# Eight state products of a chunk, written to four groups of PSUM partitions, and four copies that bring them to the next chunk

## The chip, the cores and the metric

The kernel runs on one core of a Trainium2 chip. The metric is the device time of one execution in microseconds, as the median of several runs. Each run starts from inputs in device memory and ends when the output is there.

## The reference

Two stages follow one another. The first is a state-space scan over 4 batches, 8 heads and 768 positions, with head width D = 32 and state width N = 16. Within a chunk, with `cum` the running sum of log a:

```python
L = np.exp(cum[:, :, :, None] - cum[:, :, None, :]) * causal
M = np.einsum('bhin,bhjn->bhij', Cc, Bc) * L
y = np.einsum('bhij,bhjd->bhid', M, xc) + y_inter(state)
state = decay_full * state + sum_j(Bc[j] x xc[j] * decay_from_j)
```

The second takes the scan's result as 3072 tokens of 256 values through a feed-forward layer with 2048 hidden units: `h = x @ w_in`, `g = h - tanh(h)`, `out = g @ w_out`. Everything is float32.

## The kernel before, in words

**Chunks of the scan.** The kernel cuts the 768 positions of a batch into seven chunks, six of Q = 112 positions and a last one of 96, which makes 28 chunks in all. A chunk's x tile has 128 rows (partitions): rows 0 to 15 hold the state that the chunk before left, and rows 16 to 127 its own positions. So the state enters a chunk as sixteen more rows of x, and one product over 128 rows gives both the part from the chunk and the part from the state. For each chunk:

- `chunk_a` (in the first token tile, `first_tile`) has PE compute the decay sums and the products C·B into the PSUM tile `att` (L405, L411; L346 and L357 in the first tile), ACT take the exponential into `lt` (L415, L364), DVE multiply the two (L419, L369) and GpSimd set what is not causal to zero (L422, L374).
- `chunk_y` has PE multiply `lt` and x into the PSUM tile `y` (L446): eight products, one for each head. Head h of each group of four goes to partitions 32h to 32h + 31, so that the four lie in four groups of partitions. If the chunk isn't the last of its batch, eight more products of b and x follow (L451), one for each head, 128 rows, 16 output partitions and 32 columns: the state that the next chunk needs. All eight go to partitions 0 to 15, side by side in columns 256 to 511 of `y`. 24 of the 28 chunks have them.
- Three instructions read `y`: ACT copies the state, 16 partitions and 256 columns, to rows 0 to 15 of the next chunk's x (`fn_c`, L455); ACT rounds y to float32r as `xh` (`fn_h`, L461); DVE takes the rest y - xh as `xl` (`fn_l`, L466). `y` has one buffer, so the next chunk's products wait until these are done.

**The feed-forward layer.** It works on twelve tiles of 256 tokens and eight slices of 256 hidden units (`mm1`, `act`, `mm2`). Each product is split into a high and a low part: `mm1` (L491) does xh·wh, xh·wl and xl·wh into `ph`; ACT takes the Tanh (L505), DVE subtracts (L509), ACT rounds g to gh (L513), DVE takes the rest gl (L520), and `mm2` (L541) sums three products into `o`. The weights are brought into their high and low parts by `conv` (L261 to L285) on ACT and DVE, slice by slice, beside the work on the first four token tiles. `mm2` runs two steps behind `mm1`.

**The order.** Nothing is issued as it is written down. Each piece of work is an entry `op(engine, cost, fn, r, w)` in a list, with the names that it reads and writes. `Order.schedule` then simulates the engines with the costs given and `Order.issue` does so in 16 rounds with priorities that a seeded random generator shifts by a little, one draw per entry, and issues all entries in the order of the shortest simulated span. Each engine works through its own queue in that order.

Of the kernel before, what the change touches and what calls it, by code (L numbers as in the profile page):

```python
# [21 lines left out]
NB, H, S, D, N = 4, 8, 768, 32, 16  # L22
# [10 lines left out]
CPG = 2  # L33
# [14 lines left out]
class Order:  # L48
# [12 lines left out]
    def slot(self, tag, bufs):  # L61
        k = self.count[tag] = self.count.get(tag, -1) + 1
        self.fresh[f"{tag}#{k}"] = tag, f"{tag}#{k - bufs}"
        return f"{tag}#{k}"
# [107 lines left out]
def tile_ssm_moe(ctx: ExitStack, tc: tile.TileContext, a, x, bn, bc, wts, out):  # L172
    nc = tc.nc
# [10 lines left out]
    op = Order()  # L184
    slot = op.slot
    grp = {g: {} for g in range(NG)}
# [4 lines left out]
    for t in range(NT):  # L191
        b, j = divmod(t, S // TT)
# [129 lines left out]
    def qlen(ck):  # L322
        return QL if ck % CPB == CPB - 1 else Q
# [13 lines left out]
    def first_tile():  # L337
# [39 lines left out]
        for ck in range(len(chunks[0])):  # L377
            k = chs[ck]
            k["n_l"] = op.pieces(slot("lt", NL), 2)
            if ck % CPG == 0:  # L380
                prep(ck // CPG)
            for i in range(2):
                n_f = slot("ph", NPH)
                op("PE", 0.9, lambda ck=ck, i=i: fn_f(ck, i), r=["la", "upto"], w=[n_f])
                op("ACT", 1.0, lambda ck=ck, i=i: fn_x(ck, i), r=[n_f, "ncum", "tab"], w=[k["n_l"][i]])
                if i == 0:
                    op("PE", 0.55, lambda ck=ck: fn_p(ck), r=[grp[ck // CPG]["n_bc"]], w=[n_a[ck % 2]])
                op("DVE", 0.6, lambda ck=ck, i=i: fn_m(ck, i), r=[n_a[ck % 2]], w=[k["n_l"][i]])
                op("POOL", 0.6, lambda ck=ck, i=i: fn_s(ck, i), w=[k["n_l"][i]])
            chunk_y(ck)  # L390
# [39 lines left out]
    def chunk_y(ck):  # L430

        d, k, q = grp[ck // CPG], chs[ck], qlen(ck)
        b, c = divmod(ck, CPB)
        cg = ck % CPG
        n_y = slot("y", 1)
        last = c == CPB - 1
        if c == 0:
            seq[b]["n_xh"] = op.pieces(slot("xh", 2), CPB)
            seq[b]["n_xl"] = op.pieces(slot("xl", 2), CPB)
        n_xh, n_xl = seq[b]["n_xh"][c], seq[b]["n_xl"][c]  # L440

        def fn():
            y = k["y"] = ps_y.tile([P, 2 * H * D], F32, tag="y", name=f"y{ck}")
            for hg in range(2):
                for h in range(4):
                    nc.tensor.matmul(out=y[D * h : D * h + D, hg * Q : hg * Q + q],  # L446
                                     lhsT=d["x"][:, cg, P * hg + D * h : P * hg + D * h + D],
                                     rhs=k["l"][:, 4 * hg + h, 0:q], start=True, stop=True)
            if not last:
                for h in range(H):  # L450
                    nc.tensor.matmul(out=y[0:N, H * D + D * h : H * D + D * h + D], lhsT=d["b"][:, cg, N * h : N * h + N],  # L451
                                     rhs=d["x"][:, cg, D * h : D * h + D], start=True, stop=True)

        def fn_c():
            nc.scalar.copy(grp[(ck + 1) // CPG]["x"][0:N, (ck + 1) % CPG], k["y"][0:N, H * D : 2 * H * D])  # L455

        def fn_h():
            if c == 0:
                seq[b]["xh"] = p3.tile([P, 2, S], F32R, tag="xh", name=f"xh{b}", bufs=2)
            k["yv"] = k["y"][:, 0 : 2 * Q].rearrange("p (g q) -> p g q", g=2)[:, :, 0:q]  # L460
            nc.scalar.copy(seq[b]["xh"][:, :, c * Q : c * Q + q], k["yv"])  # L461

        def fn_l():
            if c == 0:
                seq[b]["xl"] = p3.tile([P, 2, S], F32R, tag="xl", name=f"xl{b}", bufs=2)
            nc.vector.tensor_tensor(out=seq[b]["xl"][:, :, c * Q : c * Q + q], in0=k["yv"],  # L466
                                    in1=seq[b]["xh"][:, :, c * Q : c * Q + q].bitcast(F32), op=ALU.subtract)

        op("PE", 0.5 if last else 1.0, fn, r=[*k["n_l"], d["p_x"][cg], d["n_b"]], w=[n_y])
        if not last:  # L470
            op("ACT", 0.35, fn_c, r=[n_y], w=[grp[(ck + 1) // CPG]["p_x"][(ck + 1) % CPG]])
        op("ACT", 0.36, fn_h, r=[n_y], w=[n_xh])
        op("DVE", 0.4, fn_l, r=[n_y, n_xh], w=[n_xl])

# [244 lines left out]
    for i in range(4):  # L719
# [5 lines left out]
       r=[n_pq2], w=["wdec"])  # L725
# [31 lines left out]
    for ck in at_:  # L757
        plan(at_[ck][0], chunk_a, ck)
        plan(at_[ck][1], chunk_y, ck)
        if (ck + 1) % CPG == 0 and ck // CPG + NGB < NG:  # L760
            plan(at_[ck][1], group, ck // CPG + NGB)
# [58 lines left out]
```

## Time and profile before

| | us |
|---|---|
| median of 3 runs | 357.83 (356.96 to 358.04) |
| profiled execution, its own time | 358.88 |
| its span, first to last instruction | 356.9 |
| PE busy | 344.9 (97%) |
| DVE busy | 230.7 (65%) |
| ACT busy | 181.9 (51%) |
| POOL busy | 58.0 (16%) |

A page of the profile and the views of its trace all show one execution. Engines are PE (matrix products; PEld is the loading of their weights), DVE, ACT, POOL (GpSimd) and SP, which issues most DMAs. A float32 product shows as two MATMUL records and two weight loads, so that the eight state products of a chunk are 16 records. Records of PE overlap, since a product starts while the one before still runs out; busy time is the union. L451 is line 451 of the kernel.

### The profile page before, as it was taken

Reading aid. Unit: us, or ns where it says so; the run is one execution under the profiler, and the core shown is the slowest. Engines: PE = TensorE matmul, PEld = TensorE weight load, DVE = VectorE, ACT = ScalarE, POOL = GpSimd, SP = SyncE. Lnnn points to the kernel's source line nnn. Section 1 sums busy time; section 2 is a strip of 40 time slices with the busy share of each in tenths; the row PEclk is TensorE's granted clock in tenths of the full one; section 3 lists DMA queues with packets and bytes.
Section 4 is the critical chain, followed back from the end, with each engine's and each line's share of the span. In section 5 each row is a group of like instructions: output and inputs, shape, how many; then the busy total and the mean of one; then the engine's idle time right before and its main releaser. Section 6 shows DMA issues by size and latency. Waiting matters only on the chain.

```text
span 356.9 us, 8786 instructions
## 1 busy us (share of the span) xinstructions
PE 344.9 (97%) x3756; PEld 331.7 (93%) x3756; DVE 230.7 (65%) x335; ACT 181.9 (51%) x343; POOL 58.0 (16%) x69
## 2 busy tenths in 40 slices
PE   7795999999999999999999999999999999999995
PEld 6695889999999999999999999999999999999995
DVE  4879899999889665645655554644645554644552
ACT  4555687875545344355454544544544444544441
POOL 2063545401100000120211210210121110110000
PEclk9998799999999999999999999999999999999999
DMA  8877483540100001011110300300300000000000
GB/s 229 202 177 192 138 264 101 172 137 0 44 3 0 2 31 60 31 42 32 57 44 12 91 3 0 90 13 2 99 4 1 31 3 2 31 0 2 29 2 29
DMA packets 12438, 21.42 MB, mean 60 GB/s; under 512 B 2876, under 2 KB 7628, under 8 KB 12388
## 3 DMA queue, kind: packets, MB, share of 16 engines
q1 hardware_dynamic: 11824, 18.78, 18.7%
q10 hardware_dynamic: 576, 2.10, 2.0%
q8 instruction: 29, 0.48, 0.6%
q14 instruction: 9, 0.07, 0.1%
HBM read 17.55 MB, written 3.32 MB: 58 GB/s over the span
## 4 chain that ended last, share of the span: by engine, by line
PE 91%; DMA 3%; DVE 3%; ACT 1%; issue 1%; SPq 0%; ACTq 0%
PE o L541 40%; PE ph L491 38%; PE y L446 4%; DMA bc<-bc_d 3%; PE att L411 3%; PE y L451 3%; PE cp L346 2%; PE att L405 1%; DVE lt L419 1%; DVE wm L274 0%; DVE wv L278 0%; DVE lt L369 0%; PE att L357 0%; ACT wv L261 0%; DVE xl L466 0%
## 5 line engine op out<-in xcount | busy, mean ns | idle before, releaser
L509 DVE TENSOR_TENSOR g<-ph,g 128x512 f32<-128x512 f32 x96 | 66.0, 689 | 68.2 <-ACT g L505 68.1
L505 ACT ACTIVATE g<-ph 128x512 f32<-128x512 f32 x96 | 57.4, 598 | 103.4 <-PE ph L491 97.5
L491 PE MATMUL ph<-xh,wh 128*128 128x256 f32 x384 | 100.6, 284 | 0.0
L491 PE MATMUL ph<-xh,wl 128*128 128x256 f32 x384 | 99.5, 281 | 0.0
L520 DVE TENSOR_TENSOR gl<-g,gh 128x512 fp32r<-128x512 f32 x96 | 66.6, 696 | 23.8 <-ACT gh L513 21.3
L491 PE MATMUL ph<-xl,wh 128*128 128x256 f32 x384 | 76.6, 280 | 0.0
L491 PEld LDWEIGHTS ph<-xh,wh 128*128 128x128 f32 x384 | 72.6, 189 | 1.0 <-issue 0.2
L513 ACT CAST gh<-g 128x512 fp32r<-128x512 f32 x96 | 59.2, 617 | 27.5 <-DVE g L509 26.3
L491 PEld LDWEIGHTS ph<-xh,wl 128*128 128x128 f32 x384 | 72.6, 189 | 0.0
L422 POOL TENSOR_SCALAR_AFFINE_SELECT lt<-lt 128x896 f32<-128x896 f32 (+1 forms) x25 | 31.5, 1260 | 218.5 <-DVE lt L419 218.5
L541 PE MATMUL o<-gh,wh 128*128 128x256 f32 x384 | 64.0, 288 | 0.0
L541 PE MATMUL o<-gl,wh 128*128 128x256 f32 x384 | 60.7, 279 | 0.0
L541 PE MATMUL o<-gh,wl 128*128 128x256 f32 x384 | 60.6, 279 | 0.0
L491 PEld LDWEIGHTS ph<-xl,wh 128*128 128x128 f32 x384 | 59.1, 189 | 0.0
L541 PEld LDWEIGHTS o<-gh,wh 128*128 128x128 f32 x384 | 51.6, 188 | 2.7
L541 PEld LDWEIGHTS o<-gl,wh 128*128 128x128 f32 x384 | 51.9, 188 | 0.0
L541 PEld LDWEIGHTS o<-gh,wl 128*128 128x128 f32 x384 | 51.9, 187 | 0.0
L419 DVE TENSOR_TENSOR lt<-att,lt 128x896 f32<-128x896 f32 (+1 forms) x25 | 26.7, 1068 | 8.2 <-ACT lt L415 8.0
L415 ACT ACTIVATE lt<-att 128x896 f32<-128x896 f32 (+1 forms) x25 | 22.6, 902 | 9.1 <-PE att L411 6.2
L446 PE MATMUL y<-lt,x 128*32 128x112 f32 (+1 forms) x448 | 17.1, 272 | 0.0
L411 PE MATMUL att<-bc 16*128 16x112 f32 (+1 forms) x400 | 16.3, 280 | 0.0
L451 PE MATMUL y<-x,b 128*16 128x32 f32 x384 | 16.0, 197 | 0.0
(70 smaller groups left out, 252.3 us busy)
## 6 DMA issues: line engine op xcount, KB each, us to landing
raw<-w_d SPq DMA_DIRECT2D x12, 512.0 KB
x<-x_d SPq DMA_DIRECT2D x14, 256.0 KB
bc<-bc_d SPq DMA_DIRECT2D x56, 60.0 KB
out_d<-ob SPq DMA_DIRECT2D x24, 128.0 KB
raw<-w_d ACTq DMA_DIRECT2D x4, 512.0 KB
b<-bn_d SPq DMA_DIRECT2D x14, 112.0 KB
cum<-parts SPq DMA_DIRECT2D x4, 42.0 KB
lt_c<-cum SPq DMA_DIRECT2D x4, 42.0 KB
```

Source lines behind the costliest of these rows:

```text
L411: nc.tensor.matmul(out=at_[:, i, 2 + w, :], lhsT=bb[r, w], rhs=cc[r, w, 0:q], start=True, stop=True)
L415: nc.scalar.activation(k["l"][:, :, 0:q].rearrange("p (i w) q -> p i w q", i=4), k["a"][:, :, 0:2, :], AF.Exp)
L419: nc.vector.tensor_tensor(out=lt, in0=k["a"][:, :, 2:4, :], in1=lt, op=ALU.mult)
L422: nc.gpsimd.affine_select(out=k["l"][:, :, 0:q], in_=k["l"][:, :, 0:q], pattern=[[0, H], [1, q]], compare_op=ALU.is_ge, fill=0.0, base=N, ...
L446: nc.tensor.matmul(out=y[D * h : D * h + D, hg * Q : hg * Q + q], lhsT=d["x"][:, cg, P * hg + D * h : P * hg + D * h + D], rhs=k["l"][:, 4 ...
L451: nc.tensor.matmul(out=y[0:N, H * D + D * h : H * D + D * h + D], lhsT=d["b"][:, cg, N * h : N * h + N], rhs=d["x"][:, cg, D * h : D * h + ...
L491: nc.tensor.matmul(out=ph[:, j, :], lhsT=w_[:, u, 0, k, j * P : (j + 1) * P], rhs=d[("xh", "xl")[p]][:, k, ts], start=p == 0 and k == 0 an ...
L505: nc.scalar.activation(g, gs[t, u][0], AF.Tanh)
L509: nc.vector.tensor_tensor(out=g, in0=ph, in1=g, op=ALU.subtract)
L513: nc.scalar.copy(gh, gs[t, u][1])
L520: on.tensor_tensor(out=gl, in0=g, in1=gh.bitcast(F32), op=ALU.subtract)
L541: nc.tensor.matmul(out=po[t, seg][:, e, :], lhsT=w_[:, u, 1, j, e * P : (e + 1) * P], rhs=g[:, j, :], start=u == seg[0] and k == 0 and j = ...
```

## The change

The eight state products no longer go to the same 16 partitions. Product h = 2i + w now goes to partitions 32i to 32i + 15 and to columns 256 + 32w to 256 + 32w + 31 of `y`, in the order w = 0 with i = 0 to 3, then w = 1. The state of the next chunk still has to stand in rows 0 to 15 of x, head beside head. So the one copy of 16 x 256 becomes four copies of 16 x 64, each from another group of partitions to 64 columns of these rows. Each copy is an entry of its own in the planner's list, and the costs given to the planner change with it.

```diff
             if not last:
-                for h in range(H):
-                    nc.tensor.matmul(out=y[0:N, H * D + D * h : H * D + D * h + D], lhsT=d["b"][:, cg, N * h : N * h + N],
-                                     rhs=d["x"][:, cg, D * h : D * h + D], start=True, stop=True)
-
-        def fn_c():
-            nc.scalar.copy(grp[(ck + 1) // CPG]["x"][0:N, (ck + 1) % CPG], k["y"][0:N, H * D : 2 * H * D])
+
+                for w in range(2):
+                    for i in range(4):
+                        h = 2 * i + w
+                        nc.tensor.matmul(out=y[D * i : D * i + N, H * D + D * w : H * D + D * w + D],
+                                         lhsT=d["b"][:, cg, N * h : N * h + N], rhs=d["x"][:, cg, D * h : D * h + D],
+                                         start=True, stop=True)
+
+        def fn_c(i):
+            nc.scalar.copy(grp[(ck + 1) // CPG]["x"][0:N, (ck + 1) % CPG, 2 * D * i : 2 * D * i + 2 * D],
+                           k["y"][D * i : D * i + N, H * D : H * D + 2 * D])
...
-        op("PE", 0.5 if last else 1.0, fn, r=[*k["n_l"], d["p_x"][cg], d["n_b"]], w=[n_y])
+        op("PE", 0.5 if last else 0.7, fn, r=[*k["n_l"], d["p_x"][cg], d["n_b"]], w=[n_y])
         if not last:
-            op("ACT", 0.35, fn_c, r=[n_y], w=[grp[(ck + 1) // CPG]["p_x"][(ck + 1) % CPG]])
+            for i in range(4):
+                op("ACT", 0.2, lambda i=i: fn_c(i), r=[n_y], w=[grp[(ck + 1) // CPG]["p_x"][(ck + 1) % CPG]])
         op("ACT", 0.36, fn_h, r=[n_y], w=[n_xh])
         op("DVE", 0.4, fn_l, r=[n_y, n_xh], w=[n_xl])
```

## Rows read from the trace of the kernel before

**Rows 1.** The page: busy us of each engine, and the chain by engine.

```profile
PE 344.9 (97%) x3756; PEld 331.7 (93%) x3756; DVE 230.7 (65%) x335; ACT 181.9 (51%) x343; POOL 58.0 (16%) x69
...
PE 91%; DMA 3%; DVE 3%; ACT 1%; issue 1%; SPq 0%; ACTq 0%
```

**Rows 2.** Busy us of each engine in two stretches, columns in the first line.

```profile
core 0: us, PE busy (x) PEld busy (x) DVE busy (x) ACT busy (x) POOL busy (x), PEclk, DMA share, GB/s
45.00:145.00 100.00, 100.00 (x1076) 97.70 (x1076) 84.14 (x115) 58.33 (x102) 17.06 (x16) 1.00 0.23 71
145.00:353.00 208.00, 208.00 (x2286) 201.48 (x2285) 111.54 (x165) 98.70 (x182) 25.36 (x26) 1.00 0.09 27
```

**Rows 3.** The same view of three early stretches.

```profile
26.00:32.70 6.70, 3.36 (x91) 3.08 (x90) 6.66 (x9) 4.25 (x11) 1.48 (x2) 1.00 0.82 201
32.70:39.50 6.80, 6.54 (x80) 5.99 (x83) 5.85 (x8) 3.49 (x7) 4.05 (x4) 0.50 0.51 151
45.00:75.00 30.00, 30.00 (x447) 28.13 (x447) 29.13 (x38) 23.55 (x44) 13.59 (x12) 1.00 0.56 163
```

**Rows 4.** PE in order of time around one block: start us, us from first to last.

```profile
147.51 0.59 PE L446 MATMUL y<-lt,x 128*32 128x112 f32 x16
147.92 0.63 PE L451 MATMUL y<-x,b 128*16 128x32 f32 x16
148.48 0.74 PE L541 MATMUL o<-gh,wh 128*128 128x256 f32 x4
```

**Rows 5.** The state records from 45 us on: duration ns min/median/max, first and last start.

```profile
L451 PE MATMUL y<-x,b x304: 192/193/193, 45.3 to 310.4; 128*16 128x32 f32 x152
```

**Rows 6.** The block's start, view cut at 147.516, 147.62, 147.72 us; loads at 147.62.

```profile
147.51 0.28 PE L446 MATMUL y<-lt,x 128*32 128x112 f32 x1
...
147.51 0.30 PE L446 MATMUL y<-lt,x 128*32 128x112 f32 x4
...
147.51 0.40 PE L446 MATMUL y<-lt,x 128*32 128x112 f32 x8
...
147.51 0.16 PEld L446 LDWEIGHTS y<-lt,x 128*32 128x32 f32 x8
```

**Rows 7.** A block with 96 columns, its view cut at 160.93 and 161.01 us.

```profile
160.82 0.35 PE L446 MATMUL y<-lt,x 128*32 128x96 f32 x5
...
160.82 0.43 PE L446 MATMUL y<-lt,x 128*32 128x96 f32 x9
```

**Rows 8.** PE in order of time, a block at the lower clock and what follows.

```profile
37.73 1.06 PE L451 MATMUL y<-x,b 128*16 128x32 f32 x16
38.72 0.37 PE L405 MATMUL att<-rt_c,lt_c 9*128 9x224 bf16 x4
```

**Rows 9.** ACT's copies and casts by shape: busy us, mean ns, idle before.

```profile
L455 ACT COPY x<-y 16x256 f32<-16x256 f32 x24 | 8.6, 357 | 1.4 <-PE y L451 1.2
L461 ACT CAST xh<-y 128x224 fp32r<-128x224 f32 x24 | 8.2, 343 | 4.7 <-PE y L451 4.7
...
L316 ACT COPY bc<-idn 128x64 f32<-128x64 f32 x14 | 3.4, 243 | 6.5 <-DMA bc<-bc_d 6.5
...
L461 ACT CAST xh<-y 128x192 fp32r<-128x192 f32 x4 | 1.3, 316 | 0.0
```

**Rows 10.** ACT and DVE in order of time after the block at 147.5 us.

```profile
148.83 0.36 ACT L455 COPY x<-y 16x256 f32<-16x256 f32 x1
149.09 0.61 ACT L513 CAST gh<-g 128x512 fp32r<-128x512 f32 x1
149.22 0.39 DVE L466 TENSOR_TENSOR xl<-y,xh 128x224 fp32r<-128x224 f32 x1 [0.22 <-ACT x L455]
```

**Rows 11.** The first mm1 in order of time; DVE's conversion operations, mean ns second after the bar.

```profile
34.12 0.58 PE L491 MATMUL ph<-xh,wh 128*128 128x256 f32 x1
...
L285 DVE TENSOR_TENSOR wl<-wv,wh 128x1024 fp32r<-128x1024 f32 x7 | 9.6, 1371 | 0.0
L274 DVE SCALAR_TENSOR_TENSOR wm<-wv,wm 128x1024 uint32<-128x1024 uint32 x7 | 9.0, 1286 | 0.1
L278 DVE SCALAR_TENSOR_TENSOR wv<-wv,wm 128x1024 uint32<-128x1024 uint32 x7 | 8.8, 1255 | 0.0
L271 DVE TENSOR_SCALAR wv<-wv 128x1024 f32<-128x1024 f32 x7 | 6.8, 973 | 0.0
```

## The prediction

> **What bounds the kernel now.** I read the page first, then busy time by stretch, then the order of PE's work around one block of state products. The page says that PE is busy for 344.9 us of a span of 356.9, and that the chain that ended last is PE for 91% [rows 1]. The table by stretch says where that bound is strict: from 45 to 145 us PE is busy 100.00 of 100, from 145 to 353 us 208.00 of 208 [rows 2]. There every nanosecond taken out of PE's stream comes off the end, until another engine becomes the last. Before 45 us it is otherwise: from 26.0 to 32.7 us PE is busy 3.36 of 6.70 us while DVE is busy 6.66, and from 32.7 to 39.5 us PE works at a granted clock of 0.50, the lower of its two levels (1.2 GHz), after a stretch in which it was half idle [rows 3]. From 45 to 75 us DVE has only 0.87 us left of 30 [rows 3]; it is the engine to watch when PE gets faster.
>
> **The change, part by part.**
>
> *The sixteen state records of a chunk (L451 of before).* Each fp32 product shows as two MATMUL records, so eight products are 16 records. In the block at 147.5 us the first starts at 147.92 and the next work at 148.48 [rows 4]: 0.56 us. One record lasts 0.193 [rows 5], the sixteen span 0.63, so the step between starts is (0.63 - 0.193)/15 = 0.029 us: all write the first 32 PSUM partitions and go one behind the other. Fifteen steps are 0.437 us; the remaining 0.12 is what follows the last start, and it stays.
>
> *What they become.* The products for y itself (L446), just ahead of them, already go to partitions 0, 32, 64 and 96 in turn, as the state products will. Cutting the view at successive instants shows how they start: one record lasts 0.28, four together end after 0.30, so three further starts lie within 0.02 us (about 7 ns a step); eight end after 0.40 [rows 6]. So they go in rounds of four, one for each group of partitions, 7 ns apart, and a round follows the last after about 0.095 us: eight end at 0.40 and all sixteen at 0.59 [rows 4, 6], two rounds in 0.19. The round depends on the columns streamed: with 96 instead of 112 columns, five records end after 0.35 and nine after 0.43 [rows 7], a round of 0.08. Sixteen columns fewer are about 0.014 us; 80 fewer take 0.095 to between 0.02 and 0.03 us, and the step of the lone group, also of 32 columns, is 0.029. I take the measured one: a round of 0.029. Four starts of 7 ns are 0.028, so starting doesn't bound it, and weights don't either: eight weight loads of L446 have started and ended within 0.16 us [rows 6], while four matmuls started. New block: three round steps of 0.029 and three starts of 0.007, 0.109 us in place of 0.437. **Saved: 0.328 us a chunk.**
>
> From 45 us on there are 304 such records [rows 5], 19 blocks: 19 x 0.328 = **6.2 us**, all in the stretch in which PE never idles.
> Bounds for a block: nothing (the step stays 0.029), or, if the sixteen got only L446's mean step of (0.59 - 0.28)/15 = 0.021 [rows 4, 6], 0.12 us (2.3 us in all). The far end is 0.437, were they free (8.3 us). I take 0.328, from the nearest row of four groups.
>
> *Five blocks before 45 us.* One of them runs at the lower clock: from 37.73 to 38.72 us, 0.99 in place of 0.56 [rows 8], so it would save 0.328 x 0.99/0.56 = 0.58. PE isn't the strict bound here, and what follows goes through ACT and DVE. With five blocks the bounds are -1.5 (each hands its longer copies on, 0.31 below) and +2.2 (0.58 for two at the lower clock, 0.33 for three). I take +0.4: one block whose gain gets through less its copies' delay.
>
> *One copy of 16x256 becomes four of 16x64 on ACT.* The copy lasts 0.357 [rows 9], and the next ACT instruction starts 0.26 after it did [rows 10], so 0.10 of it lies under its successor. Casts from the same tile last 343 ns with 224 columns and 316 with 192 [rows 9]: 0.84 ns a column. A copy of 64 columns is then 357 - 192 x 0.84 = 195 ns; the nearest row from above is L316's copy of 64 elements, 243 ns [rows 9]. A step is 0.095 to 0.143, four are 0.38 to 0.57 of ACT instead of 0.26: **+0.12 to +0.31 us a chunk**. I take +0.15, near the row of the same tile. Over 24 chunks this is 3 to 7 us of ACT, whose cover is its idle time: 6.4 us of the 30 from 45 to 75 [rows 3], 42 of 100 from 45 to 145 and 109 of 208 after [rows 2]. On the path it costs nothing after 45 us. Queued behind the copies on ACT are the cast to gh (148.83 copy, 149.09 cast [rows 10]) and the next Tanh; for these wait DVE's two subtractions and then PE, two steps later.
> The copies also hold up DVE's xl, since it starts at the end of the copy and not of the cast to xh ahead of it: the copy ends at 149.19, xl starts at 149.22 [rows 10]. So xl, and what stands behind it on DVE (the subtraction to gl), comes later by the same 0.12 to 0.31. While DVE has idle time this is free. From 45 to 75 us it isn't quite: five blocks there would add 0.6 to 1.6 us of waiting where 0.87 is left, and PE wants its inputs 5 x 0.33 us sooner. I take 0.3 us lost (bounds 0 and 1.6 + 1.6 - 0.9 = 2.3).
>
> The rule that speaks against the copies is the Trainium skill's, page TensorEngine Tiling (Array Packing), section PSUM Bottleneck: after packing, the copy out of PSUM may become the bound. By it the copies would take part of the gain back, as in the second rival below; the trace disagrees from 145 us on, where ACT is busy 98.70 of 208 [rows 2].
>
> *The order.* All work is put in order by a planner in the kernel; 72 more entries and other costs (1.0 to 0.7 for PE, 0.35 to four times 0.2 for ACT) move its random draws, so instructions far from the change move too. Where PE idles nowhere this is worth little; before 45 us it is a gain or a loss of about one DVE conversion step, 1.3 us [rows 11], either way. I take 0.
>
> **Sum.** 6.2 + 0.4 - 0.3 = 6.3 us. The profiled execution took 358.88 us, its span 356.9 and 2.0 around it; it becomes 352.6. It stands 1.05 above the median of the three timed runs, so the time to forecast is 357.83 - 6.3 = **351.5 us**. Its own range is 349.8 to 353.3, the order's 1.3 and the copies' ends.
>
> **Rivals.**
> *The groups don't run beside each other (the change doesn't do what it says).* The state products stay at a step between 0.029 and 0.021 us, for instance since 32 columns are too short to be overlapped by the next start. For it: no row has four groups with so few columns. Against: starts 7 ns apart in L446 [rows 6]. Gain 0 to 2.3: 355.5 to 357.8, say 356.7.
> The Trainium skill has a rule that would give this, page TensorE: Matmul & The Clock Gate, section "Wait — 56ns, not 53.3ns?": start to start of matmuls never falls below about 25 ns. By it the estimate is 15 x (29 - 25) = 0.06 us a block, 1.2 in all, 356.6 us. The trace disagrees where groups differ (7 ns).
>
> *DVE or ACT takes part of it back.* PE then waits for gl between 45 and 105 us because xl waits for four copies. For it: 29.13 of 30 us busy [rows 3]. Against: after 75 us DVE has room, so only some five to seven blocks are concerned. At the upper prices: 6.2 - 2.3 - 0.3 (nothing from the early blocks, their copies late once) = 3.6, 354.2 us.
>
> *Slower: the new order delays the first mm1.* It starts at 34.12 us [rows 11], fed by DVE, which is nearly full (6.66 of 6.70 us [rows 3]). If the planner puts the second weight conversion's four large DVE operations (0.97 + 1.29 + 1.26 + 1.37 = 4.9 us [rows 11]) in front of the work that it waits for, PE idles that much longer, and a second stretch of 6.8 us at the lower clock comes on top, in which PE was busy for 6.54 [rows 3] and did half: 3.3 us. 8.2 - 6.3 = 1.9 slower, 359.7. It decides once the first mm1 starts about 5 us later, at 39, with the second stretch; without that stretch the kernel stays faster. Against it: the planner weighs this very delay in its own span.
>
> **Chances.** Forecast 0.72, part given back 0.14, groups not beside each other 0.07, slower 0.07. A measurement of this kernel tells about 0.3% (1.1 us) from no change, 356.8 to 358.9. The first two are faster, 0.86; the third lies about the lower of these lines, 0.02 faster and 0.05 the same; of the fourth 0.06 is slower and 0.01 the same. So 0.88, 0.06, 0.06. The range 349.2 to 355.2 takes in the forecast with its ends and the part given back, and leaves out the last two.
>
> **What would show it.** Right: the state records in rounds of four, sixteen starting within about 0.11 us and the next work 0.23 after the first; PE busy without a gap from 45 us on, and some 6 us less of it; four copies of about 0.2 us, 0.1 apart. Wrong: a step that stays over 0.02 us (first rival); PE waiting for DVE between 45 and 105 us (second); the first mm1 after 36 us or a second stretch at the lower clock (third). A gain above 8.3 us would mean that the order, and not the packing, did it.

## The result, and the profile after

The changed kernel takes 352.86 us (351.84 to 353.53, 4 runs) beside 357.94 for the kernel before: ratio 0.9858, interval 0.9824 to 0.9893, 5.1 us faster where 6.3 were forecast. Timed again beside the experiments it took 352.17 (ratio 0.9853, 0.9831 to 0.9874). The profiled execution took 353.53 us with a span of 351.6.

The page after, busy us of each engine:

```profile
PE 335.2 (95%) x3756; PEld 321.9 (92%) x3756; DVE 231.3 (66%) x335; ACT 192.3 (55%) x415; POOL 59.2 (17%) x69
```

Beside [rows 1], PE is busy 9.7 us less and ACT 10.4 more. The block itself, PE in order of time (start us, us from first to last), as [rows 4] before:

```profile
190.71 0.59 PE L446 MATMUL y<-lt,x 128*32 128x112 f32 x16
191.12 0.30 PE L454 MATMUL y<-x,b 128*16 128x32 f32 x16
191.35 0.72 PE L547 MATMUL o<-gh,wh 128*128 128x256 f32 x4
```

The sixteen state records span 0.30 us instead of 0.63, and the next work starts 0.23 after the first instead of 0.56. Busy us by stretch, columns as in [rows 2]:

```profile
42.50:49.50 7.00, 6.66 (x71) 6.15 (x71) 5.94 (x8) 4.75 (x12) 4.63 (x4) 0.51 0.58 188
45.00:75.00 30.00, 29.98 (x453) 27.27 (x453) 27.61 (x34) 23.25 (x54) 14.31 (x13) 0.93 0.56 167
145.00:348.00 203.00, 203.00 (x2249) 196.75 (x2248) 110.61 (x165) 103.11 (x215) 23.13 (x23) 1.00 0.09 26
```

From 145 us on PE is again never idle. From 42.5 to 49.5 us PE works at a granted clock of 0.51, the lower of its two levels, in a stretch that ran at the higher one in the execution shown of before. Ahead of it this execution has two more such stretches (0.52 from 11.5 to 25 us, 0.50 from 29.0 to 39.2), where before has one. To see where the time went, four marks serve that every execution has: the blocks of 96 columns, one for each batch. Two of them before the change, then the same two after:

```profile
241.84 0.54 PE L446 MATMUL y<-lt,x 128*32 128x96 f32 x16
...
322.86 0.54 PE L446 MATMUL y<-lt,x 128*32 128x96 f32 x16
```

```profile
239.10 0.54 PE L446 MATMUL y<-lt,x 128*32 128x96 f32 x16
...
317.61 0.54 PE L446 MATMUL y<-lt,x 128*32 128x96 f32 x16
```

The starts of the four marks, read like this from each trace, cut the span into four parts:

| us | start to mark 1 | marks 1 to 2 | marks 2 to 4 (two batches) | to the end |
|---|---|---|---|---|
| before | 49.73 | 111.09 | 162.04 | 34.0 |
| changed | 52.50 | 108.08 | 157.03 | 34.0 |
| changed, second execution | 49.77 | 110.19 | 157.03 | 34.0 |
| e1, order of before | 49.64 | 109.94 | 157.02 | 34.0 |
| e4, two groups | 47.42 | 110.08 | 159.32 | 34.0 |

The two whole batches are alike to 0.01 us in every execution of one packing: they gave 5.01 us. The parts ahead of them vary from one execution to the next, for one kernel too. Added up from the starts of single records, of the 5.01 us in e1 the steps from one state record to the next account for 3.96, and the steps among the products of `mm1` and `mm2` for 1.03.

### The profile page after: what moved, and what is told of

Its sections match the earlier page's. It is cut to its first block, busy times and chain, and to the rows that moved or that the text cites. A ratio compares the mean times of both kernels' runs of the same rounds, so it can differ in the third digit from the quotient of the medians.

```text
span 351.6 us, 8856 instructions
## 1 busy us (share of the span) xinstructions
PE 335.2 (95%) x3756; PEld 321.9 (92%) x3756; DVE 231.3 (66%) x335; ACT 192.3 (55%) x415; POOL 59.2 (17%) x69
## 4 chain that ended last, share of the span: by engine, by line
PE 92%; DMA 3%; DVE 1%; ACT 1%; issue 1%; SPq 0%; ACTq 0%
PE o L547 40%; PE ph L497 40%; PE y L446 4%; PE att L411 3%; DMA bc<-bc_d 3%; PE cp L346 2%; PE att L405 1%; PE y L454 1%; DVE lt L419 1%; SPq L209 0%; PE att L357 0%; ACT wv L261 0%; DVE wv L278 0%; ACT lt L364 0%; ACT lt L415 0%
## 5 line engine op out<-in xcount | busy, mean ns | idle before, releaser
L497 PEld LDWEIGHTS ph<-xh,wh 128*128 128x128 f32 x384 | 73.5, 191 | 1.3 <-issue 0.4
L497 PEld LDWEIGHTS ph<-xh,wl 128*128 128x128 f32 x384 | 73.6, 192 | 0.0
L459 ACT COPY x<-y 16x64 f32<-16x64 f32 x96 | 19.4, 203 | 5.5 <-DVE xl L471 4.4
L446 PE MATMUL y<-lt,x 128*32 128x112 f32 (+1 forms) x448 | 17.9, 282 | 2.8 <-issue 1.7
L312 POOL TENSOR_TENSOR b<-b,wdec 128x256 f32<-128x256 f32 x14 | 11.1, 796 | 45.4 <-DMA b<-bn_d 31.1
```

What stands on the lines that cost most here:

```text
L312: nc.gpsimd.tensor_tensor(out=b4, in0=b4, in1=wd.broadcast_to([P, CPG, H, N]), op=ALU.mult)
L497: nc.tensor.matmul(out=ph[:, j, :], lhsT=w_[:, u, 0, k, j * P : (j + 1) * P], rhs=d[("xh", "xl")[p]][:, k, ts], start=p == 0 and k == 0 an ...
```

## The experiments

My first theory, from one trace of the changed kernel: the packing gave all that was forecast, and the new order lost 2 to 3 us of it before 50 us, by the second stretch at the lower clock. The rivals were that the longer copies or the shorter PE blocks themselves lost it. Times are medians; each is beside the kernel before on the same chip, which took 357.8 to 358.06.

**e0, the changed kernel again.** No edit.

> The changed kernel again, beside the others on one chip. Both theories: 352.9 us (351.8 to 353.5), about 5 below the kernel before.

352.17 us, in line. Its trace has no stretch at the lower clock after 38.8 us, so the one from 42.5 to 49.5 in the first execution isn't part of the change.

**e1, the packing in the order of before.**

```diff
-        op("PE", 0.5 if last else 0.7, fn, ...)
+        op("PE", 0.5 if last else 1.0, fn, ...)
-            for i in range(4):
-                op("ACT", 0.2, lambda i=i: fn_c(i), ...)
+            op("ACT", 0.35, lambda: [fn_c(i) for i in range(4)], ...)
```

> Four groups and four copies, but issued in the order of the kernel before (the four copies are one entry of the planner, with its old costs). Theory 'order': the packing gives 6 to 8 us and what was lost before 50 us came with the new order, so 350 to 351.5 us, with one stretch at the lower clock near 33 to 40 us as before. Rival 'copies': the longer copies delay xl and so PE's early work, so the loss stays, 353. Rival 'clock': shorter PE blocks alone let the clock fall a second time, so 353 with a second low stretch after 40 us.

352.09 us (349.0 to 353.27), ratio 0.9828 (0.9791 to 0.9864). The interval holds the changed kernel's ratio: the new order didn't cost what I first took it to. A short stretch at the lower clock after 40 us shows here as well, as the rival 'clock' said. But the trace of e6 below, with the state products of before, has one too (41.9 to 45.3 us), and e0 has none, so it doesn't go with the packing:

```profile
29.30:36.10 6.80, 5.70 (x83) 5.22 (x80) 6.58 (x9) 4.77 (x9) 1.86 (x3) 0.50 0.60 155
36.10:42.90 6.80, 5.32 (x126) 4.76 (x125) 6.47 (x8) 5.46 (x17) 4.19 (x5) 1.00 0.75 221
42.90:46.40 3.50, 3.50 (x45) 3.17 (x44) 3.31 (x5) 2.85 (x7) 1.08 (x2) 0.51 0.09 32
```

What the trace shows besides is a new wait. PE and DVE in order of time near 70 us, two views of e1:

```profile
68.71 0.30 PE L454 MATMUL y<-x,b 128*16 128x32 f32 x16
70.02 0.39 PE L497 MATMUL ph<-xh,wh 128*128 128x256 f32 x1 [1.01 <-DVE g L515]
```

```profile
68.07 1.30 DVE L274 SCALAR_TENSOR_TENSOR wm<-wv,wm 128x1024 uint32<-128x1024 uint32 x1
69.29 1.27 DVE L515 TENSOR_TENSOR g<-ph,g 128x512 f32<-128x512 f32 x2
```

The same place in the kernel before, where PE waited for nothing:

```profile
68.14 1.30 DVE L274 SCALAR_TENSOR_TENSOR wm<-wv,wm 128x1024 uint32<-128x1024 uint32 x1
...
69.84 0.63 PE L451 MATMUL y<-x,b 128*16 128x32 f32 x16
70.40 0.38 PE L491 MATMUL ph<-xh,wh 128*128 128x256 f32 x1
```

DVE does its conversion step at 68.07 us in the one and at 68.14 in the other. PE's state block comes 1.13 us earlier (68.71 and 69.84), and then PE idles for 1.01: DVE, in whose queue the subtraction that frees `ph` stands behind the weight conversion, sets the time up to here. What set DVE's time is a second question. In e1 DVE works without a gap from 55.90 us to this subtraction, and that stretch begins with an xl that waited for the four copies on ACT:

```profile
55.90 0.39 DVE L471 TENSOR_TENSOR xl<-y,xh 128x224 fp32r<-128x224 f32 x1 [0.68 <-ACT x L459]
```

The four copies ahead of it took 0.85 us where the one copy of before takes 0.36. So by estimate up to 0.85 - 0.36 = 0.49 of the 1.01 us comes from the copies, and the rest from DVE's own queue; no run separates the two.

**e2, the new order alone.**

```diff
-            op("ACT", 0.35, fn_c, ...)
+            for i in range(4):
+                op("ACT", 0.2, lambda i=i: fn_c() if i == 0 else None, ...)
```
with the cost of PE's entry changed from 1.0 to 0.7 as in the change.

> Products into one group and one copy, as before, issued in the order of the changed kernel (three of the four copy entries issue nothing). Theory 'order': 2 to 3 us slower than the kernel before, 360 to 361 us, with the low clock again between 42 and 49 us. Rivals 'copies' and 'clock': as the kernel before, 357.5 to 358.5.

357.64 us, ratio 0.9996 (0.9975 to 1.0017). Theory 'order' falls: by itself the order costs nothing that shows, and the 2 to 3 us of the theory lie far outside the interval.

**e3, the four copies alone.**

```diff
-            nc.scalar.copy(x_next[0:N], k["y"][0:N, H * D : 2 * H * D])
+            for i in range(4):
+                s = slice(2 * D * i, 2 * D * i + 2 * D)
+                nc.scalar.copy(x_next[0:N, s], k["y"][0:N, H * D + s.start : H * D + s.stop])
```

> Products into one group as before, in the order of before, but four copies of 16x64 from those partitions. Theory 'order': 358 to 358.6 us, the copies hide. Rival 'copies': 360 or more, the early stage late by 2 to 3 us. Rival 'clock': as the kernel before.

357.95 us, ratio 1.0006 (0.9989 to 1.0023). These copies hide, and rival 'copies' falls for them. But they are quicker than those of the change. Here all four read the same 16 partitions of `y`, and in the change each reads another group. Four take 0.51 us in e3:

```profile
189.93 0.51 ACT L457 COPY x<-y 16x64 f32<-16x64 f32 x4
```

In e1 four take 0.85 (shown further below). So e3 doesn't test the change's own copies; what those cost is read from e1.

**e4, two groups in place of four.**

```diff
-                for w in range(2):
-                    for i in range(4):
-                        h = 2 * i + w
+                for w in range(4):
+                    for i in range(2):
+                        h = 4 * i + w
```
and two copies of 16x128, in the order of before.

> State products into two groups of partitions instead of four (two copies of 16x128), in the order of the kernel before. Theory 'groups': a round of two takes as long as a round of four, 0.029 us, so the sixteen starts take 7 x 0.029 + 0.007 = 0.21 us, the block 0.33 instead of 0.23; 19 x 0.226 = 4.3 us gained where PE never idles, 353 to 354 us. Rival 'any spreading': as four groups, 351 to 352. Rival 'early loss comes with packing itself': 352 to 353, since less packing loses less early.

353.68 us, ratio 0.9889 (0.9865 to 0.9912), as theory 'groups' said. The block and its successor, and the marks of two batches, are two views of e4:

```profile
177.77 0.40 PE L454 MATMUL y<-x,b 128*16 128x32 f32 x16
178.10 0.74 PE L547 MATMUL o<-gh,wh 128*128 128x256 f32 x4
```

```profile
237.16 0.54 PE L446 MATMUL y<-lt,x 128*32 128x96 f32 x16
...
316.82 0.54 PE L446 MATMUL y<-lt,x 128*32 128x96 f32 x16
```

The block takes 0.33 us, and a batch 79.66 instead of 81.02: six blocks of 0.226 are 1.36. So for two groups the dose and the gain agree to 0.01 us: a round costs 0.029 whether two groups share it or four.

**e5, e6 and e7, the clock of the early stage.** Products of constants into idle PSUM, put where PE waits, in e1, in the kernel before and in the changed kernel:

```diff
+    def fill(pool, tag, n, name):
+        pw = pool.tile([P, 4, P], F32, tag=tag, name=name)
+        one = nc.const_aps.tensor(1.0, (P, P), F32)
+        for i in range(n):
+            nc.tensor.matmul(out=pw[0:32, i % 4, :], lhsT=one[:, 0:32], rhs=one, start=True, stop=True)
...
+            if ck == 1:
+                fill(ps_y, "y", 5, "fill0")
...
+            if ck in (1, 2):
+                fill(ps_o, "po", 7 - ck, f"fill{ck}")
```

> As e1_old_order, with 16 products of constants on PE put into three gaps in which PE waits before 33 us (5 at 14 us, 6 and 5 after the state products of chunks 1 and 2; about 1.1 to 2.2 us each). Theory 'clock': the low stretch between 29 and 46 us goes or shrinks, since PE is no longer half idle ahead of it, and 1.5 to 3 us come back: 348.5 to 350. Rival 'DVE bounds the early stage': the clock rises and the time stays, 351 to 352.5. Rival 'the extra products delay': 353.

> The kernel before with the same 16 products in the same gaps. Theory 'clock, and packing makes it worse': little low clock left, 356 to 357, a smaller gain than in e5 since before lost less. Rival 'DVE bounds the early stage': 357.5 to 358.5.

> The changed kernel, its own order, with the same 16 products. Theory 'clock': 349 to 350.5, beside 352.3 without. Rival 'DVE bounds the early stage': 352.

350.93 us (0.9824, 0.9791 to 0.9857), 357.07 (0.9984, 0.9963 to 1.0006) and 351.87 (0.9847, 0.981 to 0.9883). The granted clock rose as meant, in the mean over the timed runs from 0.972 to 0.983 for e1, from 0.975 to 0.988 for before and from 0.964 to 0.981 for the changed kernel. The time followed by no more than the intervals allow for. In e5 the stretch from 26 to 33 us, at the lower clock in e1 from 29.3 us on, now runs at the higher one, and the lower one comes later, from 38.7 to 45.5 us:

```profile
26.00:33.00 7.00, 5.57 (x126) 4.94 (x126) 7.00 (x10) 4.96 (x10) 1.96 (x2) 1.00 0.82 206
```

DVE is busy 7.00 of 7.00 us in it. That the clock doesn't matter here isn't shown, though: over the 154 timed runs, each beside the mean of its own kernel and chip, a granted clock higher by 0.01 goes with a time shorter by 0.7 us (correlation -0.44). By that the three rises would be worth 0.8 to 1.2 us, which the intervals neither show nor exclude.

**e8, e9, e10 and e11, less work for DVE.** Four subtractions to gl on GpSimd; the planner's list stays as it is. e8 is e1 with this, e9 the kernel before, e10 is e5 with it, e11 the changed kernel.

```diff
-            on = nc.vector if eng == "DVE" else nc.gpsimd
+            on = nc.gpsimd if (t, u) in ((1, 0), (1, 1), (2, 0), (2, 1)) else nc.vector
```

> As e1_old_order, but four of the subtractions to gl (token tiles 1 and 2, hidden slices 0 and 1, due between 50 and 65 us) run on GpSimd in place of DVE; the planner isn't told, so the order stays. Theory 'DVE holds PE up before 70 us': the wait of 1.0 us that e1_old_order shows at 70 us shrinks or goes, and 0.5 to 1 us come back: 350.4 to 350.9 by the mean that gave 351.4. Rival 'DVE and GpSimd slow each other': DVE's operations beside it get longer, the wait stays, 351.4 to 352.5. Rival 'the early gain is lost elsewhere': the wait goes and the time stays at 351.4.

> The kernel before with the same four subtractions on GpSimd. Theory 'DVE holds PE up': PE didn't wait there, so as before, 357.3 to 358. Rival 'DVE and GpSimd slow each other': 358 to 359.

> e5_fill and e8_gl_on_pool together. Theory: 349.5 to 350.5, the lower clock's share and DVE's wait both back; if neither matters, 351.3 as e5_fill.

> The changed kernel, its own order, with the same four subtractions on GpSimd. Theory 'DVE holds PE up': 351.3 to 352, beside 352.3 without, the waits between 55 and 75 us shorter. Rival 'DVE and GpSimd slow each other': 352.3 to 353.5.

e8: 350.47 us (0.9799, 0.9769 to 0.9828). e9: 357.98 (1.0002). e10: 350.13 (0.9791, 0.976 to 0.9821). e11: 352.19 (0.9841, 0.9806 to 0.9875). The waits of PE from 45 to 95 us in e1, then in e8 (us in total, times, longest):

```profile
PE ph L497 <- DVE g L515: 1.0, 1, 1.0
```

```profile
PE ph L497 <- DVE g L515: 0.7, 1, 0.7
```

Only 0.3 of the 1.0 us came back this way. In the same order, the median of e8 is 1.6 us below e1's, but the two intervals overlap, and e8's trace owes most of it to shorter product steps (last section): between marks 1 and 2 it is 2.08 us shorter than e1's, and 1.91 of that are steps among the products of `mm1` and `mm2`. e11's trace shows no wait there at all, and its time stayed; but the first execution of the changed kernel, without this edit, shows none there either. That the wait ends with DVE's subtraction is shown, and with less work on DVE it was shorter, in one trace each (1.0 to 0.7 us, and 1.0 in e5 to 0.6 in e10); that taking it away brings the whole early gain back is not. e10 has the lowest median: its interval lies below that of the changed kernel in e0, 0.9831 to 0.9874, by a little. Its trace owes that to the short steps as e8's does (107.87 us between marks 1 and 2, beside 109.92 in e5).

## Why the prediction was right, and which of its terms were not

**The packing: right, to the 0.01 us that the views give.** Forecast were 0.109 us for sixteen starts and 0.23 us to the next work. Measured are 0.30 - 0.193 = 0.107 and 0.23, and 0.33 for two groups. The floor of about 25 ns between starts, which was the rival with the Trainium skill's rule (page TensorE: Matmul & The Clock Gate, section "Wait — 56ns, not 53.3ns?"), doesn't show where the groups differ: 0.107 us for fifteen steps is 7 ns a step in the mean.

**"19 x 0.328 = 6.2 us, all in the stretch in which PE never idles": mis-sized.** PE was never idle from 45 us on, but from 45 to 75 us DVE had only 0.87 us to spare [rows 3], and the four state blocks from 54 to 70 us are worth 1.3. The second rival had this mechanism and price (0.33 a block less DVE's slack), and I took 0.3 us for it. In e1 it is one wait of 1.01 us, and e0 has waits of 0.7 us in all between 45 and 95 us, so this sign of the second rival did appear. Its path was put only in part rightly: PE waits for the subtraction that frees `ph`, behind the weight conversion, and not for gl; that xl waits for the copies ahead of it is so, with a share of about half at most, by the estimate under e1. Between marks 1 and 2, six blocks should have given 1.97 us; e1 gave 111.09 - 109.94 = 1.15, e4 1.01 where its blocks are worth 1.36. In e1 the state records gave 1.98 and shorter product steps 0.24, and the wait and the restart after it took 1.08. The sound term is that of the two batches: 12 x 0.328 = 3.9.

**"+0.4 for the five blocks before 45 us": not seen.** Mark 1 lies at 49.73 before, at 49.77 and 52.50 in two executions of the changed kernel, 49.64 in e1 and 47.42 in e4. Executions of one kernel differ here by more than the term.

**The copies: hidden in the two batches, as forecast, but their step was mis-sized.** One copy takes 203 ns, inside my 195 to 243. I took four to be 0.38 to 0.57 us of ACT. ACT and DVE of e1 in order of time:

```profile
190.74 0.85 ACT L459 COPY x<-y 16x64 f32<-16x64 f32 x4
...
191.62 0.39 DVE L471 TENSOR_TENSOR xl<-y,xh 128x224 fp32r<-128x224 f32 x1 [0.43 <-ACT x L459]
```

Four are 0.85: these short copies follow one another with no overlap, unlike the long one before [rows 10]. The forecast's step holds where all four read the same partitions: in e3 four are 0.51, a step of 0.10. That the copies of the change read four groups in turn, as the products write them, wasn't in the sum. ACT's busy time rose by 10.4 us and not by 3 to 7 (by 3.3 in e3). In the two batches the cover held: the state records' whole 3.96 us came through in e1. Before 70 us it may not have, by the share of the wait estimated above. In the changed kernel's own order the planner puts xl between the second and the third copy in the block at 190.71 us, so that xl waits less and a copy waits for xl.

**The order: nothing that shows, as taken** (e2: 0.9996). The rival on the slow side didn't come about: the first mm1 starts at 33.53 us in the changed kernel, beside 34.12 [rows 11]. The other sign that I named for it, a further stretch at the lower clock, did show in the first execution, whose mark 1 is 2.8 us late, but not in e0; it comes and goes from execution to execution.

**A term that I didn't have: about 1.1 us from the big products.** The two batches gave 5.01 us, and twelve blocks are worth 3.94. The remaining 1.07 is in the steps of the feed-forward products (last section): added up from single starts, they are 1.03 us shorter between marks 2 and 4 in e1 than before. It came with the four groups: every trace with four has it, whatever the order, and none with one or two, neither e2 with the new order nor e3 with the four copies. Why is open. It made up for most of what DVE and the early blocks withheld: 3.9 + 1.1 + about 1 between marks 1 and 2 is 6.0 in the traces of e0 and e1, less what the early stage varies by, and 5.1 to 5.7 timed. The forecast of 351.5 was 1.4 too low, and its sum was nearer than its terms; that part is luck.

## What to carry to other kernels

Small float32 products that write the same 32 PSUM partitions went one behind the other here (0.029 us a step); spread over the four groups of partitions, four of them cost a round of one, and the fall in time could be read ahead from the step of the lone group. Count such a gain only from the point in the trace where the engine next in line has more to spare than the gain asks for: busy 100% for PE says that PE is the bound before the change, not after it. Marks that recur in every execution separate a stage that repeats to 0.01 us from one that differs by some us each time.

## What was not expected of the hardware

The same product, with the same clock granted, has two steps. Busy us from 95 to 105 us, with no block in between, in the changed kernel and then in its second execution (e0):

```profile
95.00:105.00 10.00, 10.00 (x91) 10.00 (x90) 8.94 (x14) 5.04 (x9) 0.00 (x0) 1.00 0.01 2
```

```profile
95.00:105.00 10.00, 10.00 (x87) 10.00 (x86) 8.29 (x12) 4.87 (x8) 0.00 (x0) 1.00 0.01 2
```

One engine, 10.00 us busy at clock 1.00 in both, does 91 records in the one and 87 in the other. In the starts of single records the step is 113 to 114 ns or 117 to 119 ns, and hardly anything else. A record lasts 276 ns in one state (the changed kernel from 201 to 207 us) and 279 to 280 in the other (before from 201.9 to 207.9), ns min/median/max:

```profile
L547 PE MATMUL o<-gh,wh x8: 276/276/276, 201.5 to 204.6; 128*128 128x256 f32 x8
```

```profile
L541 PE MATMUL o<-gh,wh x8: 279/280/280, 203.0 to 206.1; 128*128 128x256 f32 x8
```

A state lasts until PE next breaks off, for a block or a wait; only the first step after that can differ. In the two batches between marks 2 and 4 the count is the same in every trace of one packing: of some 1030 steps within `mm1` or within `mm2`, 302 are short in all eight traces with four groups, and 86 in all six with one or two. Over the whole span it varies: of the 2050 to 2100 steps that each trace holds, 586, 323 and 371 are short in the two executions of the changed kernel and in e1, 770 and 746 in e8 and e10, and 86 in before, in e3 and in e4. It isn't the packing alone: e2, with one group in the new order, has 361, 275 of them ahead of the batches. What sets the state at a restart stays open.

The second surprise is in the copies. A copy of 16x64 lasts 196 ns in e3 and 204 in e1, so nearly the same. The next one starts 103 to 109 ns after it in e3 (70 of 72), where all read the same 16 PSUM partitions, and 208 to 218 ns after it in e1 (71 of 72), where each reads another group. The two copies of 16x128 of e4, also from two groups, are 0.26 us apart and last 0.25. Whether it is the change of the partitions read or their distance from the partitions written isn't separated by these runs.
